# An attention and feed-forward kernel: the first chunks by halves of the heads, six chunk pairs in place of three, and a new order of the instructions

## The chip, the cores and the metric

One NeuronCore of a Trainium2 chip runs the whole kernel. Its engines are TensorE (PE in the profile, with PEld for its weight loads), VectorE (DVE), ScalarE (ACT), GpSimd (POOL) and SyncE (SP), which issues the DMAs. The metric is the device time of one execution in microseconds, smaller is better.

## The reference

A gated linear attention with a state, then a feed-forward layer:

```python
f = 1 / (1 + exp(-f_logit))                     # B, H, S, D = 4, 8, 768, 48
for t in range(S):                              # state: (B, H, D, D), from zero
    state = f[:, :, t, :, None] * state + einsum('bhd,bhe->bhde', k[:, :, t], v[:, :, t])
    y[:, :, t] = einsum('bhd,bhde->bhe', q[:, :, t], state)
x = y.transpose(0, 2, 1, 3).reshape(3072, 384)  # d_model 384, d_ff 2048
h = x @ w_in
out = (h * cos(h)) @ w_out
```

All inputs and the output are float32; the kernel multiplies in bfloat16.

## The kernel before, in words

**Chunks.** The 4 x 768 tokens are cut into 24 chunks of 128 tokens, six for each batch element. In a chunk the recurrence becomes matmuls: cumulative sums of the logarithm of the gates give a decay, q and k are multiplied by it and by its inverse, q times k gives scores under a triangular mask, scores times v and q times the incoming state give y, and k times v gives the step of the state. Two chunks make a group of one `decay` call (line 475): exp and ln of the gate logits on ScalarE, cumulative sums on TensorE (`cum`), and two exponentials (`eb`, `ei`) back on ScalarE. ScalarE changes its table between these exponentials and the cosine of the feed-forward layer (ACT_TABLE_LOAD); while a set of decays is under way, no cosine runs. The tile for gate logits (`fS`, line 375) has three buffers.

**Single chunks and pairs.** A single chunk (`attend`, line 673) loads q, k, v and f as 192 KB each, in contiguous pieces of 48 floats. A pair (`attend2`, line 577; chunk numbers of its first chunks in `DUAL`, line 294: 0, 2, 4) loads two chunks at once: partition p holds tokens 2p and 2p+1, in pieces of 96 floats, 384 KB for a tensor. Its tokens are interleaved, so it uses other masks and matmul shapes (64 rows by 64 columns for the scores, 64 rows for the state products and for scores times v), and its y comes out with tokens on the partitions: `finish` (line 559) copies it to `yb` and transposes it. A single chunk makes y already transposed, in 32-column matmuls (`pex`, line 736), and turns q and k by TensorE or, for chunks 12 to 22, by a DMA (`TURN_QK`). Chunks in pairs are written out in two DMAs of 64 partitions each (`store`, line 802).

**Feed-forward.** `moe` (line 761) runs on units of 128, 128 and then 256 tokens (`UNITS`). For each it computes `h` (w_in matmuls), the cosine on ScalarE, the product `g` on VectorE, then for each 128 tokens sixteen w_out matmuls in four ops (`o`), a copy to `ot` and the store. The weights come in four slabs of 768 KB each for w_in and w_out, through the six `gS` buffers that `gT` uses too, and are cast to bfloat16 by whichever engine the plan names (`wc`).

**The order.** Nothing is ordered by hand. Every step is an op in a `Plan` (line 115) with a cost for each engine that may run it, and a priority from the table `PR` (line 297); `PIN` (line 316) fixes the engine of some of them by their number. `Plan.run` (line 157) goes through modelled time: of the ops that could start on the engine that comes free first, within `WINDOW` nanoseconds, it takes the one with the lowest priority number. `gate` in `PR` says after how many cosines a group of decays may begin. A DMA has a modelled time on the bus (`dma=`). The program is then written in that order, and each engine runs its own list strictly in order; what the chip does differently from the plan shows as waits. q and k of a chunk share one priority, `PR["k"]`. In the trace all of this has line L257, that of the recorder through which each instruction goes, so rows are told apart by tiles: `ps` is any PSUM tile, `ld` the loads of q, k and v, `sp` the logarithm of the gates, `bi` and `b` the two decays.

Of the kernel before, what the change touches and what calls it, by code (L numbers as in the profile page):

```python
# [111 lines left out]
class Op:  # L112
    __slots__ = ("seq", "eng", "fn", "prio", "table", "deps", "vals", "alloc", "start", "end",
                 "lat", "waiting", "after", "grp", "dma", "name", "prior", "cost", "made")


class Plan:
# [3 lines left out]
    PE_LAT = 180.0  # L121
    TABLE = 1290.0
    WINDOW = 30.0
# [4 lines left out]
    def op(self, name, eng, fn, reads=(), writes=(), prio=0.0, table=None, lat=0.0, grp=None,  # L128
           dma=None):
# [4 lines left out]
        o.lat, o.grp, o.dma, o.prior = lat, grp, dma, []  # L134
# [22 lines left out]
    def run(self):  # L157
        free = {"PE": 0.0, "ACT": 800.0, "DVE": 3500.0, "POOL": 4500.0, "SP": 750.0}
        table, lock, bus, hot, pe_end = None, None, 0.0, 0.0, 0.0
# [9 lines left out]
        while len(order) < n:  # L169
            cand = []  # L170
            for o in ready:
# [18 lines left out]
                for e, cost in o.eng.items():  # L190
                    if e == "ACT" and lock is not None and o.grp != lock and o.table is not None:
                        continue
                    s = max(at, free[e] + (self.TABLE if e == "ACT" and o.table not in (None, table) else 0.0))
                    if pick is None or s + cost < pick[0]:
                        pick = (s + cost, s, e, cost)
# [19 lines left out]
            if e == "PE":  # L215
                hot *= math.exp((pe_end - s) / 2500.0)
                if hot < 0.5:
                    cost *= 1.9
                hot = 1.0 - (1.0 - hot) * math.exp(-cost / 2500.0)
                pe_end = s + cost  # L220
            o.start = s
            free[e] = s + cost
            if o.dma is not None:
                bus = max(s + cost + 700.0, bus) + o.dma
                o.end = bus + 1250.0
            else:
# [18 lines left out]


class Recorder:


    def __init__(self, engine, to):  # L250
        self._engine, self._to = engine, to

    def __getattr__(self, name):
        f = getattr(self._engine, name)

        def call(*a, **k):
            r = f(*a, **k)  # L257
            self._to.append(r.ins)
            return r
        return call  # L260


class Recorded:


    def __init__(self, nc):
        self.made = []
        for e in ("tensor", "vector", "scalar", "gpsimd", "sync"):
            setattr(self, e, Recorder(getattr(nc, e), self.made))


def apart(tc, o, base):
# [13 lines left out]
    if banks and len(others) == len(banks):  # L286
        for b in banks:
# [6 lines left out]
DUAL = [0, 2, 4]  # L294
FREE_GROUPS = 1
TURN_QK = range(12, 23)
PR = {
    "at": [-1.49, -6.93, -0.99, 13.27, -7.67, 4, 10, 9.5, -13.37, -12.55, -11.45, -9.46, -5.68, -7.15, -2,
          22.25, 10.19, 29.34, 19.9, 34.5, 43, 12.41, -1.95, 31.38],
    "dec": [-16.49, -13.88, -91.65, -10.62, -83.82, -35.17],  # L300
    "f": [-9.6, 0.04, -7, 14.37, 5.77, 13.7, 13.23, 18.93, 28.46, 33.49, 42.79, 22.57, 32.28, 13.8, 48.59,
          29.13, 41.13, 37.7, 30.11, 39.36, 49.42, 43.32, 46.86, 29.8],
    "h": [11.93, 4.6, -12.58, 7.32, -8.64, -9.43, 45, 2.23, 18.23, 18.63, 15.73, 4.41, 40.33],
    "k": [-7.62, -12.49, 0.44, 4.43, 2.7, -4.14, 7.69, 8.97, 12.29, 13.88, 14.32, 13.45, 12.51, 16.1, 9.18,
          19.51, 19.9, 19.74, 16.52, 18.13, 30.05, 34.16, 29.67, 47.94],
    "o": [14.78, 2.53, 13.63, 59.13, 65.36, 91.49, 25.09, 54.02, 36.97, 50.99, 62.96, 92.68, 123.05],
    "tq": [-17.43, -2.03, 6.77, 12.87, 14.04, 0.67, 25.22, 16.03, 47.81, 44.2, 43.57, 57.2, 54.62, 18.84,
          32.62, 19.95, 19.22, 16.34, 30.78, 4.33, 28.86, 63.13, 50.35, 20.78],
    "v": [-1.12, 8.51, 2.65, 15.87, 8.53, -6.56, 7.91, 9.09, 9.69, 12.52, 8.72, 6.57, 17.65, 13.3, 20.76,
          15.97, 19.8, 22.21, 13, 24.77, 21.05, 40.77, 28.44, 22.56],  # L310
    "w_in": [-3.97, 0.54, 2.78, 2.77],
    "w_out": [14.63, 52.89, 69.53, 73.7],
    "wc": [20.5, -34.04, -32.41, -65.79, -1.36, -30.8, -15, -24.5],
    "gate": [None, 8, 12, 14, 12, 32],
}
PIN = {1: "ACT", 9: "DVE", 11: "POOL", 13: "DVE", 28: "POOL", 29: "POOL", 32: "ACT", 46: "DVE", 48: "ACT", 51:
       "ACT", 64: "ACT", 92: "POOL", 93: "POOL", 94: "DVE", 96: "ACT", 111: "DVE", 113: "ACT", 116: "DVE", 158:
       "POOL", 161: "ACT", 173: "ACT", 176: "ACT", 178: "DVE", 220: "POOL", 223: "ACT", 237: "ACT", 239: "DVE",
       247: "ACT", 268: "DVE", 274: "ACT", 289: "POOL", 290: "POOL", 307: "ACT", 309: "ACT", 338: "DVE", 359:
       "ACT", 360: "POOL", 370: "ACT", 376: "POOL", 377: "ACT", 404: "ACT", 410: "DVE", 425: "ACT", 426: "POOL",  # L320
       434: "DVE", 440: "POOL", 441: "POOL", 450: "DVE", 471: "DVE", 477: "ACT", 492: "POOL", 508: "POOL", 509:
       "ACT", 539: "ACT", 560: "POOL", 561: "ACT", 570: "DVE", 576: "POOL", 577: "ACT", 624: "POOL", 633: "ACT",
       639: "POOL", 640: "POOL", 670: "DVE", 676: "DVE", 692: "ACT", 701: "DVE", 707: "POOL", 708: "ACT", 738:
       "DVE", 759: "ACT", 775: "ACT", 776: "ACT", 778: "DVE", 782: "ACT", 803: "ACT", 809: "ACT"}


def build(nc, cpool, ppool, q, k, v, f_logit, moe_w_in, moe_w_out, out, rec=None):
# [85 lines left out]
    P, nc = Plan(), rec or nc  # L413
    P.banks = base
    HB = lambda a: a.rearrange("p (h d) -> p h d", d=D)

    def act(n, src="P", ptr=False):
        return 0.833 * n + (160 if src == "P" else 198) + (95 if ptr else 0) - 55

# [11 lines left out]
    def load_weights(part, i, prio):  # L431
# [12 lines left out]
        P.op(f"w{part}{i}", {"SP": 420.0}, fn, writes=[stage], prio=prio, dma=2080.0)  # L444
# [7 lines left out]
    def load(t, src, b, c, n, prio, nm, eng="SP"):  # L452

        def fn(e):
            i_, o = (nc.scalar if e == "ACT" else nc.sync), t.ap
            if n not in DUAL:
                i_.dma_start(out=HB(o), in_=src[b, :, c * C:(c + 1) * C, :].rearrange("h p d -> p h d"))
            else:
                i_.dma_start(out=o.rearrange("p (h x) -> p h x", h=H),
                             in_=src[b, :, c * C:(c + 2) * C, :].rearrange("h (p e) d -> p h (e d)", e=2))  # L460
        P.op(nm + str(n), {eng: 430.0 if n not in DUAL else 500.0}, fn, writes=[t], prio=prio,
             dma=1000.0 if n not in DUAL else 1430.0)

# [11 lines left out]
    def decay(chunks, g, prio):  # L475
# [3 lines left out]
        pc = Val(scS if m == 2 else p1S)  # L479
        flat = lambda a: a.rearrange("p m h d -> p (m h d)")  # L480
        for i, (b, c, n) in enumerate(chunks[:1] if dual else chunks):
            load(ft.part((lambda a: flat(a)) if dual else (lambda a, i=i: a[:, i].rearrange("p h d -> p (h d)"))),
                 f_logit, b, c, n, PR["f"][n], "f")

        first = P.op("exp", {"ACT": act(384 * m, "S")}, lambda e: nc.scalar.activation(
            out=flat(ft.ap[:, 0:m]), in_=flat(ft.ap[:, 0:m]), func=AF.Exp, scale=-1.0),
            reads=[ft], writes=[ft], prio=prio, table="E", grp=g)
        gates.append((first, g))
        firsts.setdefault(g, []).append(first)
        loads = [w for p in ft.parts for w in p.writers]  # L490
# [3 lines left out]

        def ln(e):
# [405 lines left out]
```

## Time and profile before

| | |
|---|---|
| median of 6 runs | 194.91 us (193.59 to 195.85) |
| the profiled execution | 194.81 us |
| its span, first to last instruction | 193.0 us |
| granted TensorE clock, mean | 0.971 |
| busy: PE, PEld | 174.6, 129.0 us |
| busy: DVE, ACT, POOL | 123.4, 129.8, 75.4 us |
| DMA: read, written | 25.17, 4.72 MB |
| share of the chain that ended last | PE 66%, DMA 13%, SP's queue 7%, POOL 4% |

In the slices each digit is the busy share of one fortieth of the span, in tenths. In the windows the columns are the stretch and its length, then busy time and number of instructions of each engine, the granted clock, the mean share of the 16 DMA engines, and GB/s. A row of the timeline gives the start, the length, engine, line, operation, output and inputs, shapes and count; in brackets the idle time of the engine just before, and what ended it. The end of a matmul is modelled: matmuls overlap, so their cost is read from start to start.

### The profile page before, as it was taken

How to read it: one execution, taken by the hardware profiler on the slowest of the kernel's cores; microseconds unless marked ns; L12 is line 12 of the kernel's file. 1: busy time of each engine (PE TensorE's matmuls, PEld its weight loads, DVE VectorE, ACT ScalarE, POOL GpSimd, SP SyncE). 2: the span in 40 equal slices, each digit the busy share in tenths (PEclk: the TensorE clock that was granted, in tenths of full speed). 3: DMA queues.
4: the chain of work that ended last, by engine and by line, in shares of the span. 5: the costliest groups of instructions: out<-in, count | busy, mean ns of one | idle time of the engine just before them, and what ended most of it. 6: DMA issues, size and time to landing. Idle time of an engine off the chain costs nothing.

```text
span 193.0 us, 5285 instructions
## 1 busy us (share of the span) xinstructions
PE 174.6 (90%) x2194; PEld 129.0 (67%) x2194; DVE 123.4 (64%) x152; ACT 129.8 (67%) x163; POOL 75.4 (39%) x119
## 2 busy tenths in 40 slices
PE   0385799999999999599999999999999999999992
PEld 0263699765678866377786667876667767787651
DVE  5147689938877951459697368895388676578200
ACT  3694668987777997585869966788866552476010
POOL 8437222309831307909861696212960420000000
PEclk9998599999999999969999999999999999999999
DMA  6999999999889989799999999996132301100222
GB/s 159 298 279 315 359 246 316 172 270 301 164 179 210 207 200 190 158 223 188 226 187 214 173 238 202 223 167 163 61 82 58 84 16 41 44 0 15 77 75 82
DMA packets 106264, 33.11 MB, mean 172 GB/s; under 512 B 99584, under 2 KB 104704, under 8 KB 106240
## 3 DMA queue, kind: packets, MB, share of 16 engines
q1 hardware_dynamic: 106240, 32.78, 77.4%
q8 instruction: 17, 0.28, 0.6%
q14 instruction: 7, 0.06, 0.1%
HBM read 25.17 MB, written 4.72 MB: 155 GB/s over the span
## 4 chain that ended last, share of the span: by engine, by line
PE 66%; DMA 13%; SPq 7%; POOL 4%; issue 3%; DVE 3%; ACT 2%; DVEq 0%; POOLq 0%; ACTq 0%
PE ps L257 66%; SPq L257 7%; DMA ld<-in_v_dram 6%; DMA gT<-in_moe_w_out_dram 4%; POOL qk L257 3%; DMA ld<-in_q_dram 2%; DMA f<-in_f_logit_dram 2%; ACT cosh L257 1%; DVE w_out_bf L257 1%; DVE gT L257 1%; POOL sz L257 1%; ACT xT L257 1%; DVE vb L257 0%; ACT b L257 0%; DVE xT L257 0%
## 5 line engine op out<-in xcount | busy, mean ns | idle before, releaser
L257 ACT ACTIVATE cosh<-ps,halfpi 128x1024 bf16<-128x1024 f32 x48 | 53.3, 1115 | 24.2 <-PE ps L257 23.9
L257 PE MATMUL ps<-xT,w_in_bf 128*128 128x256 bf16 (+1 forms) x624 | 68.3, 267 | 0.5 <-ACT xT L257 0.3
L257 DVE TENSOR_TENSOR gT<-ps,cosh 128x1024 bf16<-128x1024 f32 x48 | 58.2, 1220 | 16.4 <-ACT cosh L257 14.1
L257 PE MATMUL ps<-w_out_bf,gT 128*128 128x384 bf16 x384 | 68.3, 326 | 0.4 <-DVE w_out_bf L257 0.4
L257 PEld LDWEIGHTS <-w_in_bf 128*128 128x128 bf16 x624 | 57.0, 99 | 8.7 <-DVE xT L257 0.3
L257 PEld LDWEIGHTS <-gT 128*128 128x128 bf16 x384 | 35.3, 98 | 22.9 <-issue 0.5
L257 POOL TENSOR_TENSOR qk<-ld,b 128x384 bf16<-128x384 f32 x22 | 23.2, 1067 | 23.6 <-DMA ld<-in_q_dram 10.5
L257 POOL TENSOR_TENSOR sz<-st,b 64x192 bf16<-64x192 f32 x32 | 16.1, 503 | 24.8 <-DVE st L257 23.1
L257 DVE TENSOR_TENSOR am<-ps,umask 128x1024 bf16<-128x1024 f32 x18 | 21.9, 1219 | 6.0 <-PE ps L257 5.9
L257 POOL TENSOR_TENSOR qk<-ld,bi 128x384 bf16<-128x384 f32 x22 | 22.6, 1039 | 0.2
L257 PEld LDWEIGHTS <-qk 128*128 128x128 bf16 (+1 forms) x212 | 13.0, 110 | 6.9 <-POOL qk L257 2.4
L257 POOL CAST vb<-ld 128x384 bf16<-128x384 f32 x13 | 6.6, 507 | 27.4 <-DMA ld<-in_v_dram 21.0
L257 ACT COPY ot<-ps 128x384 f32<-128x384 f32 x14 | 6.7, 484 | 13.8 <-PE ps L257 13.7
L257 PE MATMUL ps<-ident,qk 128*128 128x128 bf16 x104 | 10.0, 247 | 4.1 <-DVE qk L257 2.2
L257 ACT ACTIVATE f<-f 128x768 f32<-128x768 f32 x12 | 9.7, 840 | 5.6 <-DMA f<-in_f_logit_dram 5.5
L257 ACT ACTIVATE b<-ps 128x776 f32<-128x776 f32 x12 | 9.8, 820 | 4.3 <-PE ps L257 2.7
L257 DVE TENSOR_TENSOR st<-ps,sz 128x384 f32<-128x384 f32 x16 | 8.8, 551 | 6.0 <-PE ps L257 4.9
L257 DVE COPY ot<-ps 128x384 f32<-128x384 f32 x10 | 5.5, 554 | 9.1 <-PE ps L257 9.1
L257 PEld LDWEIGHTS <-qkt 48*128 48x128 bf16 (+2 forms) x260 | 7.0, 105 | 6.4 <-issue 2.9
L257 PE MATMUL ps<-qkt 48*128 48x128 bf16 (+1 forms) x240 | 9.8, 230 | 1.4 <-ACT qkt L257 1.4
L257 ACT ACTIVATE bi<-ps 128x768 f32<-128x768 f32 x12 | 9.8, 814 | 0.0
L257 PE MATMUL ps<-sp,incl 128*128 128x384 bf16 (+1 forms) x12 | 4.0, 378 | 6.2 <-ACT sp L257 6.2
(64 smaller groups left out, 160.4 us busy)
## 6 DMA issues: line engine op xcount, KB each, us to landing
f<-in_f_logit_dram SPq DMA_DIRECT2D x18, 192.0 KB, 4.0
ld<-in_v_dram SPq DMA_DIRECT2D x18, 192.0 KB, 4.2
ld<-in_k_dram SPq DMA_DIRECT2D x18, 192.0 KB, 3.7
ld<-in_q_dram SPq DMA_DIRECT2D x18, 192.0 KB, 3.6
out_dram<-ot SPq DMA_DIRECT2D x18, 192.0 KB, 1.9
gT<-in_moe_w_in_dram SPq DMA_DIRECT2D x4, 768.0 KB, 7.6
gT<-in_moe_w_out_dram SPq DMA_DIRECT2D x4, 768.0 KB, 7.4
f<-in_f_logit_dram SPq DMA_DIRECT2D x3, 384.0 KB, 5.9
```

The lines of the kernel that those rows point to most:

```text
L257: r = f(*a, **k)
```

## The change

- `DUAL` goes from 0, 2, 4 to 0, 2, 4, 6, 8, 10: twelve chunks are loaded and computed as pairs.
- New `HALVED = [0, 2]`: for these two pairs f, k and q are loaded in two DMAs of four heads each, and exp, ln, `cum`, `eb` and `ei` are done once for each half; the product of q or k with the decay waits for its half alone.
- The plan's model: `PE_LAT` 180 to 150, a new `FORM` of 96 ns when a matmul op has another tile shape than the one before it, `WINDOW` 30 to 200, DMA times of 1050, 1500, 2130, 1600 and 545 in place of 1000, 1430, 2080, 1800 and 520, and SP held back when more than three DMAs are under way; other PE costs for several ops.
- New numbers in `PR` (priorities and gates) and in `PIN`.
- The last 128 tokens' output is computed, copied and stored in 256 and 128 columns.
- The recorder classes are replaced by a callback that collects the instructions.

```diff
-    PE_LAT = 180.0
+    PE_LAT = 150.0
+    FORM = 96.0
-    WINDOW = 30.0
+    WINDOW = 200.0
...
+                    if e == "PE" and o.form[0] != form:
+                        s = max(at, free[e] + self.FORM)
...
                 o.end = bus + 1250.0
+                sent.append(bus)
+                if len(sent) > 3:
+                    free[e] = max(free[e], sent[-4] + 900.0)
...
-DUAL = [0, 2, 4]
+DUAL = [0, 2, 4, 6, 8, 10]
+HALVED = [0, 2]
...
-    "dec": [-16.49, -13.88, -91.65, -10.62, -83.82, -35.17],
+    "dec": [-40.13, -18.23, -118.54, -46.76, -113.79, -51.74],
-    "f": [-9.6, 0.04, -7, 14.37, 5.77, 13.7, 13.23, 18.93, 28.46, 33.49, 42.79, 22.57, 32.28, 13.8, 48.59,
+    "f": [-33.54, 19.93, -13.27, 40.85, 11.69, 33.17, 10.24, 7.48, 19.13, 35.33, 34.56, -8.91, 83.83, 25.67,
...
-    "k": [-7.62, -12.49, 0.44, 4.43, 2.7, -4.14, 7.69, 8.97, 12.29, 13.88, 14.32, 13.45, 12.51, 16.1, 9.18,
+    "k": [-19.36, -9.86, -11.55, -8.7, 12.98, 15.54, 17.61, 50.25, 24.91, 19.36, 19.87, 27.13, 50.07, 53.19,
...
-    "v": [-1.12, 8.51, 2.65, 15.87, 8.53, -6.56, 7.91, 9.09, 9.69, 12.52, 8.72, 6.57, 17.65, 13.3, 20.76,
+    "v": [-13.3, 8.45, -11.68, 3.43, 13.02, 15.37, 13.49, 28.89, 25.51, 21.76, 19.22, 48.22, 37.19, 43.36,
...
-    "w_in": [-3.97, 0.54, 2.78, 2.77],
-    "w_out": [14.63, 52.89, 69.53, 73.7],
+    "w_in": [-7.72, -4.28, -1.16, -0.96],
+    "w_out": [9.87, 4.13, 4.15, 9.92],
-    "gate": [None, 8, 12, 14, 12, 32],
+    "gate": [None, 8, 3, 13, 20, 23],
...
+    def load(t, src, b, c, n, prio, nm, flat=lambda a: a):
...
+        m = 2 if n in HALVED and nm != "v" else 1
+        for i in range(m):
+            w = H // m
+            dst = t.part(lambda a, i=i: flat(a)[:, i * HD:(i + 1) * HD]) if m == 2 else t
+            P.op(nm + str(n), {"SP": 470.0}, lambda e, i=i, w=w, dst=dst: nc.sync.dma_start(
+                out=(dst.ap if m == 2 else flat(dst.ap)).rearrange("p (h x) -> p h x", h=w), in_=src[
+                    b, w * i:w * i + w, c * C:(c + 2) * C, :].rearrange("h (p e) d -> p h (e d)", e=2)),
+                writes=[dst], prio=prio + 0.01 * i, dma=1500.0 / m)
...
+        halved = chunks[0][2] in HALVED
+        for part in ([0], [1]) if halved else (list(range(m)),):
+            s, w = slice(part[0], part[-1] + 1), len(part)
+            of = lambda v, i=part[0]: v.parts[i] if halved else v
...
+            first = P.op("exp", {"ACT": act(384 * w, "S")}, lambda e, s=s: nc.scalar.activation(
+                out=flat(ft.ap[:, s]), in_=flat(ft.ap[:, s]), func=AF.Exp, scale=-1.0),
+                reads=[of(ft)], writes=[of(ft)], prio=prio, table="E", grp=g)
...
-                    reads=[src, dec], writes=[parts[j][i]], prio=prio)
+                    reads=[v.parts[i] if v.parts else v for v in (src, dec)], writes=[parts[j][i]], prio=prio)
...
+            pieces = [(0, d_model)] if r0 + C < n_tokens else [(0, 256), (256, d_model)]
+            for a, z in pieces:
+                po, half = Val(p1S), ot.part(lambda o, a=a, z=z: o[:, a:z]) if len(pieces) > 1 else ot
```

## The prediction, made before the changed kernel ran

> **What bounds the kernel now.** I read the page's slices first, then the table of windows, then the timeline of the three places where TensorE (PE) isn't full. The slices:
>
> ```profile
> PE   0385799999999999599999999999999999999992
> PEclk9998599999999999969999999999999999999999
> DMA  6999999999889989799999999996132301100222
> ```
>
> A slice is 4.8 us. PE is full from about 24 us to 189 us but for one dent near 80 us, and the dent is also where the granted clock drops. The DMA engines are full for the first 130 us. So the end is set by the sum of PE's work, plus three losses: the start, the dent, the tail. The windows give the losses a size:
>
> ```profile
> 0.00:23.30 23.30, 11.54 (x182) 9.05 (x182) 12.30 (x29) 14.52 (x17) 12.76 (x30) 0.89 1.07 280
> 15.00:25.00 10.00, 6.66 (x123) 5.54 (x116) 7.37 (x10) 5.01 (x6) 5.06 (x6) 0.66 1.13 334
> 48.00:60.00 12.00, 11.86 (x228) 8.87 (x228) 9.97 (x14) 9.23 (x15) 6.52 (x12) 1.00 0.92 178
> 78.00:88.00 10.00, 7.71 (x139) 5.64 (x137) 5.50 (x9) 8.02 (x13) 5.31 (x8) 0.83 0.91 192
> 100.00:110.00 10.00, 10.00 (x119) 6.32 (x118) 5.65 (x8) 8.68 (x12) 3.06 (x5) 1.00 1.21 195
> ```
>
> Columns: length, busy PE, weight loads, DVE, ACT, POOL, then clock, DMA share, GB/s. **Start:** PE is busy for 11.5 of 23.3 us, much of it at half clock; at full clock I put that work at 7.5 us, so about 15.8 us are lost. **Dent:** 2.3 us of idle in 78:88, and a clock of 0.83 over 10 us is 1.7 us more: about 4.0 us. **Tail:** from the last matmul's end (189.6) to the end of the span: 3.4 us. The start in the timeline:
>
> ```profile
> 4.42 0.84 ACT L257 ACTIVATE f<-f 128x768 f32<-128x768 f32 x1 [2.41 <-DMA f<-in_f_logit_dram]
> ...
> 8.71 0.56 DVE L257 TENSOR_TENSOR qk<-ld,b 128x384 bf16<-128x384 f32 x1 [4.00 <-ACT b L257]
> ...
> 12.48 0.56 DVE L257 CAST vb<-ld 128x768 bf16<-128x768 f32 x1 [1.94 <-DMA ld<-in_v_dram]
> ...
> 23.31 2.27 PE L257 MATMUL ps<-xT,w_in_bf 128*128 128x128 bf16 x24
> ...
> 26.63 1.46 ACT L257 CAST w_in_bf<-gT 128x1536 bf16<-128x1536 f32 x1
> ```
>
> The gate logits land at 4.4, the first product at 8.7 waits for the decay, v lands at 12.5, the first feed-forward matmul comes at 23.3, the last w_in slab at 26.6. The dent:
>
> ```profile
> 79.24 0.84 ACT L257 ACTIVATE f<-f 128x768 f32<-128x768 f32 x1 [3.11 <-DMA f<-in_f_logit_dram]
> ...
> 80.87 0.32 PE L257 MATMUL ps<-sp,umask 128*128 128x384 bf16 x1 [1.99 <-ACT sp L257]
> ```
>
> ScalarE waits 3.1 us for a gate-logit load, holding the exp table; PE waits for ScalarE. The sum below is against the profiled run, 194.81 us: span 193.0 and 1.8 around it. The median of the runs is 194.91, practically the same.
>
> **Three more pairs (chunks 6 to 11): PE pays.** At full clock both forms stand side by side:
>
> ```profile
> 41.91 0.33 PE L257 MATMUL ps<-sp,incl 128*128 128x384 bf16 x1
> ...
> 42.34 0.32 PE L257 MATMUL ps<-sp,incl 128*128 128x384 bf16 x1
> ...
> 42.77 0.32 PE L257 MATMUL ps<-sp,umask 128*128 128x384 bf16 x1
> ...
> 43.03 0.32 PE L257 MATMUL ps<-sp,umask 128*128 128x384 bf16 x1
> ```
>
> From start to start, a pair's cumulative sums cost 2 x 0.43 = 0.86 us, two single chunks' 2 x 0.26 = 0.52: +0.34. State products: 0.45 (48.11 to 48.56) against 2 x 0.17: +0.11. Scores: 0.58 against 2 x 0.33: -0.08. Outputs: 0.94 (52.26 to 53.20) against 2 x 0.50: -0.06. Transposes of q and k: 16 either way. New are six transposes of yb, 0.18 + 0.26 (54.28, 54.63): +0.44. Together +0.75 a pair, **+2.2 us** for three. They lie in a stretch where PE has nothing to hide them under, so they count in full. Two yb copies a pair (0.48 on ACT, 0.55 on DVE) replace two small vz casts (0.30); in the windows these engines have idle time for that.
>
> **What the pairs save in DMA.** In 48:60, single loads alone, the engines move 178 GB/s at a share of 0.92, that is 193 GB/s when busy: 1.02 us for 192 KB. In the first 5 us, pair loads almost alone, it is 162 at 0.67, or 242: 1.63 us for 384 KB. Three pairs of four tensors save 12 x (2.04 - 1.63) = 4.9 us of DMA time. Here a rule speaks against the change: the Trainium skill, "DMA: Bandwidth & Descriptors", in its table of figures at the top, wants at least 512 B in a piece for line rate. A pair's pieces are 384 B (two tokens of 48 floats), still below, so by the rule alone the saving could be nil; by the rows it is 4.9 us. I take the rows. But it is worth time only where PE waits for a load: at the dent. Otherwise it is hidden. The output of these chunks leaves as two DMAs of 96 KB: six more issues, some 0.6 us each on SP, against twelve fewer load issues: the queue gains.
>
> **Halves of the heads in the first two pairs.** Half the gate logits land about 0.7 us earlier (192 KB at 280 GB/s), at 3.7. ScalarE's 128x768 passes take 0.84; copies of 384 and 768 (0.51, 0.83) say 0.2 fixed, so a half is 0.52. Of the 4.29 us from 4.42 to 8.71, exp and ln give back 0.32 each, the sums 0.75 (only one half is waited for), the exponential 0.34: 2.56 remain, and the first product moves from 8.7 to about 6.3. Price: four more fixed parts a pair, 1.6 us of ScalarE, and six more load issues of 0.46 (row of 0.74 us) on SP: 2.8 us. Both lie beside waits for DMA; SP's issues of 1.4 to 3 us at 6 to 11 us show that the queue is held back by the engines, not by its own work. Without that cover the 2.8 us would delay w_in by as much.
>
> **The new order at the start.** By the priorities f, k, q, v of both pairs go ahead of all of w_in; so v of the first pair comes after 1.57 MB, not 2.75. From the first landing (0.39 MB at 4.4) and 280 GB/s it lands at 4.4 + 1.18/0.28 = 8.6, not 12.5, and the first copy of qkt no longer queues behind a w_in cast. But w_in moves the other way: its last slab lands after eight pair loads and four slabs, 6.2 MB, where it had nine before, 6.6 MB: 1.4 us earlier only, and its first slab lands later (about 18, against 11). So the first feed-forward matmul comes near 20, not at 16 where attention would allow it, and PE is fed by w_in slab by slab. The gain is between 1.4 (the last slab) and 4 (the chain), taken as **-2.5 us**; the bounds are +1.5 (the weights hold PE back more than the chain gains) and -5. On the clock a row and a rule differ: the column says 1.00 from 5 to 15 us, yet the sums of 6.94 and 7.21 us start 0.27 apart, against 0.16 at 41.91. The skill's "TensorE: Matmul & The Clock Gate", part 1, says that half rate is the default until about 3.4 us of sustained work have passed. The durations follow the rule. By the column an earlier start would be worth its full 4 us; by the durations part of the early work runs at half rate: one more reason to stay at 2.5.
>
> **The dent.** The new gates and priorities spread the decay groups, and f of chunks 4 to 11 needs half the issues. Whether the load of chunks 14 and 15 (single before and after; three f buffers) is still late can't be read from the diff. Bounds: the whole 4.0 gained, or 3 lost to a new wait of this kind. I take 60%: **-2.4 us**.
>
> **Tile shapes.** At 99.95 us twelve w_in matmuls take 1.40 us to the first score matmul, where 12 x 0.109 are 1.31: a change of shape costs 0.09. The order has 86 changes. The plan now charges 96 ns each and may choose within 200 ns rather than 30. If it merges one in ten: **-0.8 us**; bounds 0 and -2.
>
> **Tail.** The last output is cut in 256 and 128 columns. The last copy shrinks from 0.48 to about 0.27 and its DMA from 192 to 64 KB (about 0.3 us): -0.5; sixteen more short matmuls cost about 0.1. **-0.4 us.** The Recorder that goes away acts on no engine: nothing.
>
> Sum: 194.8 + 2.2 - 2.5 - 2.4 - 0.8 - 0.4 = **190.9 us**.
>
> **Rivals.** (1) *Weights hold the start back*: no gain there, 193.4. For it: DMA is full from 5 to 25 us, and w_in is what PE waits for in the end. Against it: PE idles for attention, not for weights, until 21 us. (2) *The dent only moves*: -2.4 falls away, 193.3. With both, 195.8, no change. (3) *A new hole, slower*: pair 4 and w_out now compete for the DMA right after w_in. PE's stock then is the feed-forward of four chunks, 21 us (96 w_in matmuls at 0.055 and 48 at 0.109, 64 w_out at 0.163), so with what is left of attention it lasts to about 45 us. If w_out (3.1 MB, 11 us) goes first, pair 4's loads land near 41 and its chain (8.7 to 21.5 in the first pair) ends at 52 or so. It decides from an x of pair 4 later than 45: 5 us of idle and one to two spells of half clock as at 83 us (1.7 each, say 2.6): 190.9 + 7.6 = 198.5; half that hole gives 194.7. Against it: pair 4's own matmuls fill 4 us, and w_out needs stage buffers that gT takes too.
>
> **Chances.** Forecast 0.55; one of the small rivals (1, 2) 0.20; both, or half the hole, 0.07; the hole 0.18. What this kernel's measurement can tell from no change is about 0.5% (193.9 to 195.9). That gives faster 0.75, same 0.07, slower 0.18. The range runs from 187 (start -4, whole dent, tile shapes -1.5) to 196.5, into a hole of 5 us.
>
> **What would show it.** Right: the first product near 6.3, v cast near 9, the first w_in matmul near 20, a PE row without a digit below 9 after slice 5, clock 0.9 in 78:88, 36 transposes of yb instead of 18. Wrong: a hole in 35 to 55 us with a fall of the clock, a wait of PE for ScalarE's sp that is longer than 2 us anywhere, a first w_in matmul after 23, or fewer than 2.2 us added by the pairs.

## The result and the profile after

The changed kernel takes 192.82 us (median of 34 runs, 191.96 to 195.07), the kernel before 194.15 in the same comparison (69 runs): ratio 0.9945, 95% interval 0.9928 to 0.9963. Forecast were 190.9 us, 2.0% less; measured is 0.55% less. The direction was right and the size was not; the rival "the dent only moves" (193.3 us) is nearest to what came. Ratios, here and below, leave out executions more than 1.5% above the fastest of their kernel (half of the twelve of before_late), medians do not, so the two can differ a little (192.82 / 194.15 would be 0.9931).

The slices of the profile after (a slice is 4.8 us):

```profile
PE   0688998999999999998899999999999999999993
PEclk9999999999999999999999999999999999999999
DMA  5999999989979999998999999973592101011122
```

The dent at slice 16 and its fall of the clock are gone. In their place PE has an 8 in slices 6, 18 and 19 (counted from 0), and the DMA engines are full to slice 25. The windows after, in the columns used before:

```profile
60.00:70.00 10.00, 9.60 (x75) 6.98 (x74) 6.57 (x6) 8.53 (x10) 1.64 (x3) 1.00 1.05 228
70.00:80.00 10.00, 9.70 (x132) 6.41 (x130) 7.95 (x11) 8.51 (x12) 4.33 (x6) 1.00 0.95 192
80.00:90.00 10.00, 9.40 (x180) 7.54 (x181) 8.80 (x11) 8.82 (x11) 5.34 (x8) 1.00 0.92 190
90.00:100.00 10.00, 9.06 (x121) 7.34 (x118) 7.43 (x10) 6.77 (x10) 6.32 (x8) 1.00 0.99 194
60.00:100.00 40.00, 37.76 (x493) 28.27 (x492) 30.74 (x37) 32.64 (x41) 17.63 (x25) 1.00 0.98 201
```

And the same 40 us of the kernel before:

```profile
60.00:100.00 40.00, 37.45 (x453) 28.48 (x450) 25.92 (x30) 31.59 (x41) 21.40 (x30) 0.96 0.97 198
```

PE idles for 2.24 us of these 40 after and for 2.55 before. One hole of 2 us has become a spread of small ones; what really went is the half clock (0.96 to 1.00). The waits of PE from 28 to 140 us after (engine, tile and line that waits, what ended the wait: us in all, times, longest) show what the small ones wait for:

```profile
PE ps L727 <- POOL qk L679: 0.7, 1, 0.7
PE ps L657 <- POOL sz L549: 0.6, 1, 0.6
PE ps L776 <- DVE gT L786: 0.5, 1, 0.5
PE ps L604 <- DVE qk L585: 0.5, 2, 0.3
PE ps L507 <- ACT sp L496: 0.4, 1, 0.4
```

No single wait is over 0.7 us. The timeline after, behind the first of them:

```profile
83.21 2.56 SPq L807 DMA_DIRECT2D out_dram<-ot  x2
...
85.60 1.00 POOL L679 TENSOR_TENSOR qk<-ld,b 128x384 bf16<-128x384 f32 x1 [2.21 <-DMA ld<-in_q_dram]
85.81 0.59 SPq L438 DMA_DIRECT2D ld<-in_k_dram  x1
86.44 0.69 SPq L438 DMA_DIRECT2D ld<-in_q_dram  x1
...
90.89 1.00 POOL L679 TENSOR_TENSOR qk<-ld,b 128x384 bf16<-128x384 f32 x1 [1.33 <-DMA ld<-in_q_dram]
...
93.35 0.34 PE L727 MATMUL ps<-vb,qk 128*128 128x96 bf16 x4 [0.69 <-POOL qk L679]
```

SP issues a store of output, then k and q of chunk 12; q lands 4.29 us after its issue, POOL makes two products and a cast, and PE gets its operand at 93.35. Before, PE waited at 80.9 for ScalarE, which waited for a load of gate logits. The names differ, the end of both chains is a load. The start after, row for row:

```profile
3.26 0.52 ACT L484 ACTIVATE f<-f 128x384 f32<-128x384 f32 x1 [1.25 <-DMA f<-in_f_logit_dram]
...
6.50 0.56 DVE L585 TENSOR_TENSOR qk<-ld,b 128x384 bf16<-128x384 f32 x1 [1.77 <-DMA ld<-in_q_dram]
...
9.38 0.82 POOL L432 CAST vb<-ld 128x768 bf16<-128x768 f32 x1 [0.42 <-DMA ld<-in_v_dram]
...
20.62 1.22 PE L776 MATMUL ps<-xT,w_in_bf 128*128 128x128 bf16 x12
...
25.53 1.46 POOL L432 CAST w_in_bf<-gT 128x1536 bf16<-128x1536 f32 x1
```

**An account of the span.** From the trace I sum every matmul at its own full-clock spacing (0.162 us for 384 columns, 0.109 for 256, and so on) and every change of tile shape at 0.094 us. What the time exceeds this sum by is called lost: idle, half clock, or waits too short to be listed. The row of the matmuls is thus counted, not timed; what the matmuls of the pairs cost beyond these spacings stands in the rows of losses. "Again" is a second profiled execution of the changed kernel (the experiment after_again).

| us | before | after | again | forecast change |
|---|---|---|---|---|
| lost up to 30 us | 17.72 | 14.83 | 14.83 | -2.5 |
| lost from 30 to 100 us | 5.62 | 4.91 | 5.90 | -2.4 |
| lost from 100 us to the last matmul | 0.38 | 0.96 | 1.00 | 0 |
| matmuls | 157.48 | 159.68 | 159.68 | +2.2 |
| changes of tile shape (86, 79, 79) | 8.08 | 7.43 | 7.43 | -0.8 |
| last matmul to the end | 3.74 | 3.33 | 3.54 | -0.4 |
| span | 193.03 | 191.14 | 192.39 | -3.9 |

One row fails: the middle. It gave 0.7 in one execution and took 0.3 in the other, where 2.4 were expected. Split up, the 5.62 us before are 3.09 us of idle (windows of 30 to 60 and 60 to 100), about 1.7 of half clock and 0.8 that are neither; after, 3.01, none and 1.9; again, 4.00, none and 1.9. So the half clock went, the idle did not, and 1.1 us of the last kind came. In the profiles without half clock in this stretch that last part is 1.6 to 2.0 us with six pairs (six profiles) and 0.7 to 1.2 with three (tail_only, before_late, before_late_tail). My estimate from this is that the three new pairs cost PE nearer to 3 us than 2.2; no run separates it.

### The profile page after: what moved, and what is told of

Same layout as the page of the kernel before. It is cut to its first block, busy times and chain, and to the rows that moved or that the text cites. A ratio compares the mean times of both kernels' runs of the same rounds, so it can differ in the third digit from the quotient of the medians.

```text
span 191.1 us, 5431 instructions
## 1 busy us (share of the span) xinstructions
PE 176.5 (92%) x2276; PEld 131.5 (69%) x2276; DVE 131.5 (69%) x169; ACT 127.1 (66%) x162; POOL 70.1 (37%) x109
## 3 DMA queue, kind: packets, MB, share of 16 engines
q1 hardware_dynamic: 94096, 32.78, 73.4%
## 4 chain that ended last, share of the span: by engine, by line
PE 65%; DMA 10%; ACT 6%; issue 5%; POOL 5%; DVE 4%; SPq 3%; POOLq 0%; ACTq 0%; DVEq 0%
PE ps L798 27%; PE ps L776 24%; DMA ld<-in_q_dram 8%; PE ps L752 2%; PE ps L604 2%; DMA ld<-in_v_dram 2%; PE ps L714 2%; SPq L446 2%; ACT cosh L783 2%; POOL sz L549 1%; DVE qk L585 1%; DVE gT L786 1%; ACT bi L524 1%; SPq L807 1%; PE ps L507 1%
## 5 line engine op out<-in xcount | busy, mean ns | idle before, releaser
L798 PE MATMUL ps<-w_out_bf,gT 128*128 128x384 bf16 (+2 forms) x400 | 67.9, 320 | 0.4 <-DVE xT L460 0.4
L717 DVE TENSOR_TENSOR am<-ps,umask 128x1024 bf16<-128x1024 f32 x12 | 14.5, 1214 | 6.7 <-ACT bi L524 3.7
L460 DVE COPY ot<-ps 128x384 f32<-128x384 f32 x12 | 6.5, 552 | 16.5 <-PE ps L798 16.4
L460 ACT COPY ot<-ps 128x384 f32<-128x384 f32 (+2 forms) x13 | 5.8, 456 | 16.4 <-PE ps L798 16.3
L623 DVE TENSOR_TENSOR am<-ps,pmask 128x1024 bf16<-128x1024 f32 x12 | 14.4, 1220 | 2.3 <-PE ps L617 2.2
L484 ACT ACTIVATE f<-f 128x768 f32<-128x768 f32 (+1 forms) x14 | 10.5, 748 | 4.8 <-DMA f<-in_f_logit_dram 4.8
L432 POOL CAST vb<-ld 128x384 bf16<-128x384 f32 (+1 forms) x13 | 7.8, 606 | 15.5 <-DMA ld<-in_v_dram 12.0
L524 ACT ACTIVATE b<-ps 128x776 f32<-128x776 f32 (+1 forms) x14 | 10.1, 723 | 3.3 <-PE ps L513 1.7
L679 POOL TENSOR_TENSOR qk<-ld,bi 128x384 bf16<-128x384 f32 x12 | 12.0, 1002 | 0.0
L496 ACT ACTIVATE sp<-f 128x768 bf16<-128x768 f32 (+1 forms) x14 | 10.5, 752 | 0.4
L524 ACT ACTIVATE bi<-ps 128x768 f32<-128x768 f32 (+1 forms) x14 | 10.0, 717 | 0.0
L604 PEld LDWEIGHTS <-qk 128*128 128x128 bf16 x96 | 7.0, 113 | 3.4 <-POOL qk L585 1.1
```

The source lines that it names most:

```text
L460: (nc.scalar.copy if e == "ACT" else nc.vector.tensor_copy)(out=o, in_=i_)
L484: first = P.op("exp", {"ACT": act(384 * w, "S")}, lambda e, s=s: nc.scalar.activation(out=flat(ft.ap[:, s]), in_=flat(ft.ap[:, s]), func=A ...
L524: nc.scalar.activation(out=out_.ap[:, s, :], in_=pc.ap.rearrange("p (m n) -> p m n", m=w)[:, :, 0:n], func=AF.Exp, scale=sign)
L604: nc.tensor.transpose(out=o[:, j, :, p, x, :], in_=twin(j, 2 * i + p, x), identity=ident)
L623: P.op("am", {"DVE": dve(1024)}, lambda e, sc=sc, am=am: nc.vector.tensor_mul(out=am.ap.rearrange("p r a n -> p (r a n)").rearrange("p (a ...
L679: P.op("qk", {"POOL": 1020.0}, lambda e, j=j, src=src, dec=dec: E(e).tensor_mul(out=qkv()[:, j, :, 0:D], in0=HB(src.ap), in1=HB(dec.ap[:, ...
```

## The experiments

In the experiments the order of each engine's instructions is written out as a list and kept, except for the edit: `Sa12.k12.0` is an item, S for SP (P, A, D, G for PE, ScalarE, VectorE, GpSimd), then the op, here the load of k of chunk 12; d stands for decays, a for attention, m for the feed-forward unit from that token on. The runs stand in four comparisons (four, four, three and one of the rows below), each with its own executions of the kernel before, which took 196.3 to 196.7 us there, 1.1 to 1.3% more than above, so ratios are what compares. The changed kernel itself is 0.55% faster above and 1.0% in after_again, and its two profiles have 2.24 and 3.10 us of idle from 60 to 100 us: a difference of less than half a per cent between comparisons, or of less than 1 us of idle between two single profiles, is not read here. The table has their profiles: losses as above, PE's idle time from the windows.

| run | median us | ratio to before | span | lost to 30 | lost 30 to 100 | idle 60 to 100 |
|---|---|---|---|---|---|---|
| halves_only | 196.53 | 0.9981 [0.9945, 1.0017] | 196.6 | 18.2 | 8.7 | 4.03 |
| halves_undone | 197.83 | none | 195.1 | 17.4 | 6.2 | 3.23 |
| tail_only | 195.60 | 0.9935 [0.9894, 0.9976] | 192.4 | 18.0 | 5.0 | 2.90 |
| before_f_early | 197.01 | 1.0020 [0.9988, 1.0052] | 194.8 | 18.3 | 6.8 | 3.45 |
| after_again | 194.11 | 0.9896 [0.9857, 0.9935] | 192.4 | 14.8 | 5.9 | 3.10 |
| loads_swapped | 195.09 | 0.9893 [0.9833, 0.9953] | 193.2 | 15.2 | 6.5 | 3.39 |
| pieces_48 | 200.45 | 1.0204 [1.0150, 1.0258] | 199.1 | 14.9 | 11.5 | 5.55 |
| start_and_tail | 195.64 | 0.9953 [0.9918, 0.9988] | 192.5 | 16.1 | 6.9 | 0.40 |
| stores_late | 190.21 | 0.9704 [0.9662, 0.9747] | 188.6 | 14.9 | 2.9 | 0.55 |
| late_and_loads | 193.16 | 0.9865 [0.9819, 0.9911] | 192.6 | 15.4 | 6.3 | 3.64 |
| before_late | 195.14 | 0.9848 [0.9800, 0.9897] | 191.7 | 18.3 | 1.5 | 0.05 |
| before_late_tail | 191.33 | 0.9751 [0.9702, 0.9800] | 189.7 | 18.6 | 2.0 | 0.51 |

The profiled execution of halves_only took 198.34 us, 1.8 above its median, so only its start is read. For halves_undone there is no ratio: its four executions spread from 195.6 to 199.6 us, and only its profile is read. The median of before_late is 0.8% under that of the kernel before in its comparison (196.66 us), its ratio 1.5%.

### The start: halves, order, or both

**halves_only**, the kernel before with halves in the first two pairs, and its own order.

```diff
-HALVED = []
+HALVED = [0, 2]
```

> The kernel before, each engine's order kept, with only the halves of the heads added in the first two pairs (two loads each for f, k and q; exp, ln and the two exponentials in halves). Theory A: the halves alone shorten the first chain (first product near 6.3 us instead of 8.7), but v of the first pair and w_in keep their old places in SP's queue, so the first w_in matmul stays within 0.7 us of 23.3 and the time falls by 0 to 1 us (ratio 0.995 to 1.0). Rival B: the halves carry most of the 2.9 us that the start gained: first w_in matmul near 21, ratio 0.985 to 0.99. The stretch 70 to 90 us is untouched here and shows whether the half-clock spell at 83 us comes again: if it was an accident of the one profiled execution, the clock of 80 to 90 is 1.0.

The first rows of its timeline that matter:

```profile
7.15 0.56 DVE L683 TENSOR_TENSOR qk<-ld,b 128x384 bf16<-128x384 f32 x1 [2.43 <-ACT b L622]
...
13.85 0.56 DVE L530 CAST vb<-ld 128x768 bf16<-128x768 f32 x1 [5.67 <-DMA ld<-in_v_dram]
...
24.13 1.97 PE L874 MATMUL ps<-xT,w_in_bf 128*128 128x128 bf16 x24
```

The first product comes 1.6 us earlier than before (8.71), but v of the first pair, issued behind a slab of w_in in that order, lands no earlier (cast at 13.85, before 12.48), and the first feed-forward matmul at 24.13, before 23.31. The time is that of the kernel before; its interval leaves room for a gain of 0.5% at most.

**halves_undone**, the changed kernel with whole loads and whole exponentials in its first two pairs, in the new order.

```diff
-HALVED = [0, 2]
+HALVED = []
```

> The changed kernel, each engine's order kept, with whole loads and whole exponentials in the first two pairs. Theory A: the new place of v and w_in in the queue carries the start, so about 1 us of its 2.9 is given back: 0.5 to 1.5 us slower than the changed kernel (ratio to before 0.997 to 1.002). Rival B: the halves carry it: 2.5 to 3.5 us slower than the changed kernel (ratio 1.007 to 1.013).

Lost up to 30 us are 17.4, against 14.8 with the halves and 17.7 before: by this one profile the new order alone gives 0.4 of the 2.9. The first product is at 8.90 and the first feed-forward matmul at 23.15. So the start's gain belongs to neither part: the order brings v early, the halves bring the decay early, and attention needs both.

### The tail

**tail_only**, the kernel before with the last output in two pieces.

```diff
-Am2816.ot.1
+Dm2816.ot.1
+Pm2816.o.8
+Pm2816.o.9
+Pm2816.o.10
+Pm2816.o.11
 Sm2816.st_o.1
+Am2816.ot.2
+Sm2816.st_o.2
```

> The kernel before with only its last 128 tokens' output cut in 256 and 128 columns. From the two profiles the time from the start of the last matmul to the end falls by 0.4 us: ratio 0.997 to 0.9985, the last copy 0.27 instead of 0.48 us. If the sixteen additional matmuls cost as much as the shorter tail gives, 1.0. It is also one more sample of the dent at 78 to 88 us of the kernel before: idle of about 2.3 us there, with or without a half-clock spell.

From the last matmul to the end it takes 3.04 us, against 3.74: -0.7 where the forecast said -0.4 and the changed kernel showed -0.4 and -0.2. The ratio, 0.9935, is a little more than 0.7 us explains (0.9964), within its interval. Its profile has no half clock from 60 to 100 us, although PE idles there for 2.90 us.

### The middle: is it the order?

**before_f_early** takes the wait that the forecast named at its root: in the kernel before, the gate logits of chunks 14 and 15 are issued ahead of a load of q and a store.

```diff
-Sa10.q10.0
...
-Sm512.st_o.0
...
+Sd14.f15.0
+Sd14.f14.0
+Sa10.q10.0
+Sm512.st_o.0
...
-Sd14.f15.0
...
-Sd14.f14.0
```

> The kernel before with one edit to SP's order: the gate logits of chunks 14 and 15 are issued ahead of the q load of chunk 10 and of one output store, not behind them. Theory A: the dent is the late landing of these logits alone; they go out about 2 us earlier, PE's idle time in 70 to 90 us falls from 2.3 to under 0.8 us, a half-clock spell there goes with it: 1.5 to 3.5 us faster (ratio 0.982 to 0.992). Rival B: the DMA engines are full in that stretch, so what is brought forward delays the next load, and the idle time comes back within 15 us as a wait for q or k: within 0.7 us of before.

Windows of before_f_early:

```profile
70.00:80.00 10.00, 9.00 (x83) 5.84 (x80) 3.82 (x7) 8.60 (x12) 4.05 (x5) 1.00 0.92 200
80.00:90.00 10.00, 8.36 (x158) 5.95 (x155) 6.99 (x9) 8.62 (x13) 6.94 (x9) 1.00 0.93 197
90.00:100.00 10.00, 9.19 (x119) 7.45 (x120) 6.41 (x9) 5.64 (x8) 7.54 (x12) 0.83 1.07 193
```

The wait for ScalarE falls from 2.0 to 1.2 us, a wait of 1.9 us for GpSimd's `sz` appears, and the half clock comes 8 us later. Idle in 60 to 100 is 3.45 us, not less than before (2.55), and the time is the same: what one load gains, another loses.

**loads_swapped** tries the same on the changed kernel: k and q of chunk 12 and three more loads that come late change places with loads that have time.

```diff
-Sa17.k17.0
+Sa12.k12.0
...
-Sa17.q17.0
+Sa12.q12.0
...
-Sa23.v23.0
+Sa13.q13.0
...
-Sa16.v16.0
+Sa14.q14.0
...
-Sa14.q14.0
+Sa16.v16.0
...
-Sa17.v17.0
+Sa13.k13.0
...
-Sa12.k12.0
+Sa17.k17.0
...
-Sa12.q12.0
+Sa17.q17.0
...
-Sa13.k13.0
+Sa17.v17.0
...
-Sa13.q13.0
+Sa23.v23.0
```

> The changed kernel with five loads exchanged in SP's queue, buffers with them: k and q of chunk 12 against those of chunk 17, q of 14 against v of 16, k and q of 13 against v of 17 and of 23. The displaced ones are used 20 to 50 us later. Theory A: the changed kernel's idle time at 85 to 95 us comes from the order of the loads (these five are used when they land, others lie for 20 us and more); it falls by 1 to 1.5 us, ratio to the changed kernel 0.992 to 0.996. Rival B: the idle time is conserved, since the next load or ScalarE or GpSimd is late by as much: within 0.4 us of the changed kernel.

**after_again** is the changed kernel once more, without an edit, on the same chip.

> The changed kernel as it is, with its order of instructions written out, as the yardstick of the three others on the same chip, and as a second sample of its trace. Theory A (idle time of PE in 30 to 100 us is set by when loads land, not by accident): idle in 60 to 100 us 2.2 us within 0.4 again, at the same instructions. Rival B (accident of one execution): the waits of 0.5 to 0.7 us at 89 and 93 us are absent or elsewhere. Ratio to before 0.993 to 0.997.

```profile
60.00:100.00 40.00, 36.90 (x485) 27.61 (x483) 29.89 (x37) 32.37 (x40) 17.49 (x25) 1.00 0.96 199
```

Its idle is 3.10 us, outside the 2.2 within 0.4 that I expected, and its ratio is lower than expected; the waits are mostly the same ones, up to 1.0 us long.

Windows of loads_swapped:

```profile
80.00:90.00 10.00, 9.95 (x190) 7.80 (x187) 8.18 (x12) 8.67 (x12) 6.33 (x10) 1.00 0.87 184
90.00:100.00 10.00, 7.38 (x101) 6.10 (x99) 6.37 (x9) 6.21 (x9) 4.90 (x7) 1.00 0.97 188
```

80 to 90 is now full, and the idle stands in 90 to 100 as one wait of 2.4 us for GpSimd's product. In sum 3.39 us, against 3.10 in after_again, with the same ratio: no gain of the 1 to 1.5 us that theory A promised.

**start_and_tail** gives the kernel before the new start (halves and order of the first 20 us) and the new tail, without the three more pairs: its list has the first two pairs, w_in and the first feed-forward ops in the order of the changed kernel, all else in its own.

```diff
-HALVED = []
+HALVED = [0, 2]
```

> The kernel before with the changed kernel's first 20 us (halves, and the loads and casts of the first four chunks and of w_in in the new order) and its tail; no further pairs, and from then on the order of before. Theory A: the start's 2.9 us survive to the end, and the pairs' 2.2 us aren't paid: 3 us faster than before, ratio 0.982 to 0.987, better than the changed kernel. Rival B: the middle is set by when loads land, and the loads after w_in land no earlier than before; PE's head start at 30 us is waited away by 60 to 95 us: ratio 0.995 to 1.0 and idle time in 30 to 95 us larger by 2 to 3 us.

Windows, then waits of PE, of start_and_tail:

```profile
30.00:60.00 30.00, 25.85 (x312) 18.10 (x312) 21.60 (x24) 19.72 (x27) 12.73 (x15) 0.94 1.04 238
60.00:100.00 40.00, 39.60 (x506) 30.39 (x505) 28.23 (x32) 34.52 (x43) 21.37 (x32) 1.00 0.93 192
```

```profile
PE ps L897 <- DVE w_out_bf L531: 2.3, 1, 2.3
PE ps L875 <- DVE gT L885: 1.8, 1, 1.8
```

And the row of VectorE behind the first of these waits:

```profile
44.63 1.46 DVE L531 CAST w_out_bf<-gT 128x1536 bf16<-128x1536 f32 x1 [4.70 <-DMA gT<-in_moe_w_out_dram]
```

At 30 us PE is 1.6 us ahead of the kernel before, at 60 us it is 3.3 behind (22.1 lost against 18.8), waiting for w_out among others, at 95 us it is level (22.9 against 23.2), the dent of 60 to 100 being nearly gone. PE came sooner and stood sooner, for a slab of w_out. But this list keeps the old place of w_out, whose last two slabs SP issues at 38.6 and 40.4 us (in the changed kernel all four are issued by 22 us). So the run does not tell full DMA engines from a late place in the queue. Three reorderings, and none made the loss up to 100 us less by more than the 1 us that two executions of one kernel differ by.

### The middle: is it the DMA engines?

**pieces_48** keeps the pairs 6, 8 and 10 and their compute, but moves their q, k, v and f in pieces of 48 floats, two DMAs of 192 KB for each tensor, as single chunks do.

```diff
+                if n < 6:
+                    nc.sync.dma_start(out=o.rearrange("p (h x) -> p h x", h=w),
+                                      in_=s_.rearrange("h (p e) d -> p h (e d)", e=2))
+                    return
+                for x in range(2):
+                    nc.sync.dma_start(out=o.rearrange("p (h e d) -> e p h d", e=2, d=D)[x],
+                                      in_=s_.rearrange("h (p e) d -> e p h d", e=2)[x])
```

> The changed kernel with the loads of pairs 6, 8 and 10 done in pieces of 48 floats again (two DMAs of 192 KB each, alternate tokens), everything else the same: what the pairs' larger pieces are worth without their matmuls. Theory A: 4 to 6 us more DMA time in 25 to 70 us, where loads already run 3 us behind the plan, make PE wait: 2 to 5 us slower than the changed kernel, and the pairs' 2.2 us of PE are thus paid back. Rival B: the saving is hidden (loads of the second half of the program fill the queue anyway): within 0.7 us.

A window of pieces_48, and its longest wait of PE:

```profile
70.00:80.00 10.00, 5.84 (x39) 3.51 (x38) 3.73 (x5) 8.40 (x11) 3.07 (x4) 0.67 0.94 195
```

```profile
PE ps L611 <- ACT sp L600: 4.2, 1, 4.2
```

The engines' time for all DMAs rises by 3.6 us (73.8% of 199.1 against 74.5% of 192.4), and the span by 6.7: a hole of 4.2 us behind a late load of gate logits, and 10.2 us at half clock. Without its larger pieces the changed kernel, in its own order, is 2% slower than the kernel before, more than the 2 to 5 us over the changed kernel that theory A gave. (Twelve more issues on SP are part of this edit, and the DMA time of the changed kernel's two profiles itself differs by 3 us: 73.4% of 191.1 and 74.5% of 192.4.)

**stores_late** takes DMA time out of the full stretch in another way, with nothing else changed: the first seven stores of output go out at about 150 us, where the engines are a quarter busy.

```diff
-    otS = slots("ot", 4, [128, d_model], F32)
+    otS = slots("ot", 12, [128, d_model], F32)
...
-Sm128.st_o.0
...
-Sm0.st_o.0
...
 Sm1792.st_o.1
+Sm128.st_o.0
+Sm0.st_o.0
+Sm256.st_o.0
+Sm256.st_o.1
+Sm768.st_o.0
+Sm512.st_o.0
+Sm768.st_o.1
```

> The changed kernel with its first seven stores of output (128 tokens each, 1.3 MB in all, issued from 38 to 84 us) moved to 150 us, behind the fourteenth to be stored; ot has 12 buffers in place of 4 for that. Every engine but SP keeps its order, nothing is left out. Theory A (up to about 95 us the DMA engines are full, and the time at which loads land sets what PE waits for): some 7 us of DMA time are taken out of the full stretch, so loads land earlier, and of PE's 2.2 us of idle from 60 to 100 us at least 1.5 go; the span falls by 1.5 to 2.5 us against the changed kernel (ratio to the kernel before about 0.98). Rival B (the idle is set by the order on the engines, by POOL, ScalarE and the exp table, not by the DMA engines): idle in 60 to 100 us stays within 0.5 of 2.2, and the time is that of the changed kernel.

Slices of PE, then windows, of stores_late:

```profile
PE   0588998999999999999999999999999999999993
```

```profile
60.00:70.00 10.00, 10.00 (x84) 7.45 (x83) 6.66 (x6) 9.20 (x11) 1.09 (x3) 1.00 0.59 123
70.00:80.00 10.00, 9.75 (x135) 6.44 (x133) 8.47 (x12) 7.93 (x11) 4.54 (x6) 1.00 0.87 166
80.00:90.00 10.00, 9.95 (x201) 8.06 (x199) 8.44 (x12) 9.43 (x13) 6.63 (x10) 1.00 0.96 189
90.00:100.00 10.00, 9.75 (x108) 7.39 (x106) 9.16 (x12) 7.86 (x12) 5.58 (x8) 1.00 0.92 177
60.00:100.00 40.00, 39.45 (x519) 29.33 (x517) 32.73 (x40) 34.42 (x45) 17.85 (x26) 1.00 0.83 164
```

The DMA share of 60 to 70 falls to 0.59, PE's idle in 60 to 100 from 3.10 (after_again) to 0.55, the span from 192.4 to 188.6, more than the 1.5 to 2.5 us expected. 3.0 of these 3.8 us are lost time of 30 to 100 us. SP issues q of chunk 12 at 82.2 us, where the changed kernel did at 86.4. This is the fastest kernel of the study: 0.9704 of the kernel before, 2% less than the change itself (0.9896 in after_again).

**late_and_loads** puts as many bytes back: where each of the seven stores was, SP issues loads of a piece of w_in into a spare tile. They wait for no copy of output.

```diff
+                    def dummy(e, dm=dm, r0=r0):
+                        for x in range(2):
+                            nc.sync.dma_start(out=dm.ap[64 * x:64 * x + 64],
+                                              in_=moe_w_in[r0 // 8 + 64 * x:r0 // 8 + 64 * x + 64, 0:d_model])
```

> As the run before it, but where each of the seven stores was issued, SP now issues loads of as many bytes (two of 64 rows by 384 columns of w_in in float32) into a spare tile that nobody reads; they wait for no copy. So the DMA engines carry as much as in the changed kernel, but SP's queue never waits for a copy of output. It adds reads that the reference doesn't need. Theory A1 (it is the bytes on the full DMA engines): the idle in 60 to 100 us comes back to about 2.2 us, time that of the changed kernel within 0.4%. Theory A2 (it is SP, in order, held by stores that wait for copies of output, with loads behind them): the idle stays low, time that of the run with late stores alone.

Windows of late_and_loads:

```profile
90.00:100.00 10.00, 7.50 (x102) 6.26 (x102) 5.79 (x9) 5.74 (x9) 6.27 (x9) 1.00 1.00 193
60.00:100.00 40.00, 36.36 (x475) 27.35 (x474) 29.33 (x36) 31.86 (x40) 16.64 (x24) 1.00 0.96 188
```

The share is 0.96 again, the idle 3.64 us, the ratio 0.9865 (after_again 0.9896). (The profiled execution, 194.47 us, is the slowest of its six, so its idle may be on the high side.) The twelve buffers of ot stayed. So neither these buffers nor stores that wait for copies of output, and hold up SP's queue with loads behind them, are what costs; the transfers ahead of the loads are. Bytes and the number of issues came back together here, so how much belongs to each was not told apart.

### What the larger pieces are worth then

**before_late**, the kernel before with its first eight stores moved behind `m1792.st_o.1`, by the same edit.

> The kernel before with its first eight stores (62 to 83 us) moved to 130 us or so, behind the fifteenth to be stored; ot has 12 buffers. Theory A: the dent of the kernel before falls too, 1.5 to 3 us of idle and half clock from 60 to 100 us, ratio 0.985 to 0.992, that is, more than the changed kernel gained by its new order in the middle (0.7 us). Rival B: the waits stay where they are (ScalarE for f of chunks 14 and 15, PE for sp), ratio within 0.4% of 1.

Windows, then two rows of the timeline, of before_late:

```profile
60.00:100.00 40.00, 39.95 (x511) 30.00 (x508) 30.02 (x34) 35.03 (x44) 22.76 (x33) 1.00 0.98 181
```

```profile
75.97 1.59 ACT L581 ACTIVATE f<-f 128x768 f32<-128x768 f32 x2
...
156.92 0.40 PE L811 MATMUL ps<-qkt 48*128 48x128 bf16 x8 [2.15 <-DMA qkt<-qk]
```

The dent is gone: 0.05 us of idle, no half clock, lost from 30 to 100 us 1.5 against 5.6. The exponential of the gate logits, which stood until 79.24 for its load, now runs at 75.97 without a wait. Yet the DMA share of the stretch is 0.98, as before: the engines are as full, but with other loads, and those that PE needs land earlier. But I had put the stores ahead of the last two transposes of q and k by DMA, and PE waits 2.15 us for one of them. Its times scatter (192.1 to 197.4).

**before_late_tail** puts the same stores behind the last transpose and adds the new tail.

```diff
 Sa22.tq.0
+Sm128.st_o.0
+Sm256.st_o.0
...
+Sm768.st_o.1
```

> The kernel before, with three pairs, whole loads and its own order, in which only two things are altered: its first eight stores of output go out behind the last transpose of q and k by DMA (about 153 us; ot has 12 buffers), and its last output is cut in 256 and 128 columns. Theory A (with the early stores gone from the full stretch PE waits for no load, so the three more pairs are then a price of 2.2 us on PE without a return, and all that the halves and the new order still give is their 2.9 us at the start): 0.05 us or so of idle from 60 to 100 us as in the run that moved these stores alone, the 2.2 us hole near 155 us of that run gone, tail 0.5 to 0.7 shorter: span 188.5 to 189.5, ratio 0.968 to 0.977, level with the changed kernel with late stores (0.9704). Rival B (the larger pieces are what the middle needs in any case): a new wait for a load of more than 1 us between 60 and 130 us, ratio 0.98 or more.

Windows of before_late_tail:

```profile
60.00:100.00 40.00, 39.49 (x507) 29.70 (x505) 29.25 (x33) 34.29 (x44) 23.09 (x33) 1.00 1.00 186
130.00:180.00 50.00, 50.00 (x593) 36.32 (x591) 31.33 (x32) 27.26 (x35) 11.15 (x15) 1.00 0.30 80
```

The hole is gone, the span 189.7 (a little over the 189.5 expected, with 0.51 us of idle in place of 0.05), the ratio 0.9751, with an interval that overlaps that of stores_late. The rival, a new wait for a load of more than 1 us, did not come. So the old order with three pairs, and two small edits, beats the changed kernel. That it comes near stores_late is a balance: stores_late loses 3.7 us less up to 30 us, and its six pairs cost the 2.2 to 3 us of PE that this kernel doesn't pay. With the stores put off, nothing here shows a return for the three new pairs; the new start with three pairs and late stores, w_out early, was not run.

## Why the prediction was wrong, point by point

**The failed step: "The dent. ... I take 60%: -2.4 us".** I treated the hole as a matter of order: one load late, one engine holding the exp table, and new priorities that spread the groups. The half clock in it did go (about 1.7 us), but the idle of 60 to 100 us did not (2.55 before, 2.24 and 3.10 after). What the runs show in its place is that PE there waits for loads with other transfers ahead of them. Moving single loads forward (before_f_early, loads_swapped) moved the wait and did not lessen it. Taking seven or eight stores, 1.4 to 1.6 MB, out of the stretch removed it in both kernels (3.10 to 0.55 us, 2.55 to 0.05), and as many bytes put back restored it (3.64). That the DMA engines are full is not enough to make PE wait: they are in before_late (0.98) too. The middle gave -0.7 us in one execution and +0.3 in the other.

**The sentence that hid it: the DMA saving "is worth time only where PE waits for a load: at the dent. Otherwise it is hidden".** The forecast counted the dent once, for the order, and gave the saved DMA time nothing of its own. pieces_48 shows that the changed kernel's order lives on that saving: without it 6.7 us of span are lost. That it is spent on keeping the start's 2.9 us is my reading and not shown, since start_and_tail, which waits them away, also has w_out late. The saving itself was put too high: 4.9 us forecast, 3.6 in the totals of pieces_48 against after_again, 3.8 from the packet times in the profile after (15.5 ns for 192 B, 26.0 for 384 B, by 16 engines). The rule on small pieces that I weighed there, and set aside for the rows, would by my reading have made it nil; the rows were nearer.

**The half clock in the 4.0 us, and the base.** The 1.7 us of half clock vary with the execution: from 60 to 100 us 3.4 us at half clock in the profiles before and before_f_early, none in tail_only. Over the 25 executions of the kernel before in the first comparison the mean granted clock runs from 0.964 to 1.0; in the 34 of the changed kernel it is 0.99 or more. So this part of the forecast came, by and large, and the idle is what failed. The base was high as well: the profiled 194.81 us is 0.7 above the median of the 69 executions.

**Right: the start** (-2.5 forecast, -2.9 in both profiles). First product 6.50 (forecast 6.3), v cast 9.38 (8.6 to 9), first feed-forward matmul 20.62 (20). What I did not see is that the terms aren't additive: halves alone nothing, order alone 0.4.

**The pairs**: the 36 transposes of yb are there, and the account gives +2.20, but from the same spacings as the forecast; the losses of the middle suggest nearer +3. **Right: tile shapes** (-0.8; 79 changes in place of 86 are -0.65 at the 0.094 us of a change, which no run tested by itself). **Right: the tail** (-0.4, measured -0.41 and -0.20; alone -0.7).

**Not foreseen:** 0.6 us more are lost after 100 us, in both executions of the changed kernel. 0.4 of them are one wait of PE for an `xT` of VectorE (at 139 us in the profile after); the rest was not followed up.

**The signs I had named.** "A PE row without a digit below 9 after slice 5" failed, and was the right thing to look at. The hole in 35 to 55 us did not come, and after the start no wait of PE for `sp` is over 0.4 us in the profile after (0.9 in after_again).

## What to carry to other kernels

Where an engine idles now and then for loads, and the DMA share is near 1, ask what is transferred ahead of those loads before you count on a new order: here moving single loads moved the idle, and putting other transfers off to a slack stretch removed it, though the share stayed near 1 in one kernel. Look first for transfers that nobody waits for, such as stores of output; putting seven of them off cost eight more output buffers and gave 2%, more than the whole change. And a gain early on is kept only if the next bound lets it through, so ask of each saving what it would be worth alone.

## What the runs showed of the hardware that I had not expected

- **Half-clock spells come and go with the execution.** In the profiles they last 3.4 us or twice that (before 6.8 from 18.1 and 3.4 from 83.0; before_f_early 3.4; pieces_48 6.8 and 3.4; start_and_tail 3.4). A 2.0 us wait was followed by one in the kernel before, and in before_f_early one followed waits of at most 1.3 us; a single wait of 2.4 us in loads_swapped was not followed by one. The Trainium skill, "TensorE: Matmul & The Clock Gate", part 1, speaks of a free-running window of about 3.4 us, which fits the lengths and the chance.
- **Twice the bytes in a piece for 1.7 times the time.** In the profiles of before and after a piece of 192 B takes 15.5 to 16.4 ns on its DMA engine, one of 384 B 26 to 27.5, both under the 512 B that I had read as the size that counts. Moving three pairs' loads back to the smaller pieces, with twelve more issues, took the ratio from 0.99 to 1.02.
